# The opening of batch 0: idle matmul counts, the place of two transpose groups, and the place of one product group

## The chip, the core and the metric

The kernel runs on one core of one Trainium2 chip. A core has a matrix engine (TensorE, with its weight loads shown apart in the profile as PEld), VectorE (DVE), ScalarE (ACT), GpSimd (POOL) and SyncE (SP), each of which takes its instructions in order from its own program, and 16 DMA engines that bring data from the chip's main memory. Engines tell each other of finished work through semaphores. The metric is the time of one execution on the device, in microseconds (us), as the median of several runs. Results of matmuls go to a memory of their own, PSUM, from where VectorE or ScalarE must copy them before a matmul or a DMA can use them.

## The reference

Linear attention with a cosine reweighting, followed by a feed-forward layer; q, k and v have shape (8, 8, 576, 64) in float32, that is 8 batches, 8 heads, 576 positions and 64 features.

```python
def _attn_ref(q, k, v):
    theta = np.pi / 2.0 * pos / S
    def phi(x, c, s):
        r = np.maximum(x, 0.0)
        return np.concatenate([r * c, r * s], axis=-1)
    q_p = phi(q, cos_w, sin_w)
    k_p = phi(k, cos_w, sin_w)
    kv = np.einsum('bhsf,bhsd->bhfd', k_p, v)
    z = np.sum(k_p, axis=2)
    num = np.einsum('bhsf,bhfd->bhsd', q_p, kv)
    den = np.einsum('bhsf,bhf->bhs', q_p, z)[..., None] + 1e-06
    return (num / den).astype(np.float32)

def _moe_ref(x, w_in, w_out):
    h = x @ w_in
    g = h * (1.0 / (1.0 + np.exp(-1.702 * h)))
    return (g @ w_out).astype(np.float32)
```

The attention's output is laid out as 4608 rows (batch and position) of 512 columns (head and feature); w_in is 512 x 2048 and w_out 2048 x 512. The output is 4608 x 512 in float32.

## The kernel before

The kernel goes through the eight batches one after the other. For each batch it makes the features of k and q (relu, times a cosine and a sine, function `trig`), the matrix k^T v with the column sums of k beside it (`kv_mm`, copied out of PSUM by `kv_evac`), the quotient for five chunks of 128 positions (`num_mm` on TensorE, `num_div` on VectorE), a transpose of the quotient (`xturn_mm` on TensorE and `xturn_evac` on ScalarE in batch 0), and then the two layers (`mm1` with `gelu`, `mm2`). In the steady part the attention of the next batch is placed among the matmuls of the present one, so TensorE always has work. There is no scheduler: each engine's order is the order in which the kernel's text calls it (`manual_schedule`), and the semaphore waits follow from the tiles that an instruction reads and writes.

Batch 0 has no earlier batch to hide behind. Its order is written out by hand from line 375 to line 415:

- `idle` issues matmuls on a tile of zeros, whose results nobody reads: 12 with 512 columns, 100 with 64 columns (lines 375 and 376), and three more with 512 columns at line 392.
- The features of k (`trig(kr, kf, j)`, j = 0 to 8) are shared between VectorE and ScalarE (`act=True`).
- Line 385 makes the column sums of k, with `ones` as the moving side: 72 matmuls of one column.
- `qturn_pe(c)` transposes the features of q for chunk c on TensorE: 8 transposes, 4 for c = 4. `qevac(c)` copies them to `qT`, on VectorE, or on ScalarE with `act=True`. Transposes and the products of the first layer share a pool of four PSUM buffers (`pmm`, tiles named `mm`); tiles are given out in turn, so turn 3 takes turn 0's buffer and turn 4 takes turn 1's.
- `kv_mm(0, 2, ...)` and `kv_mm(2, 4, ...)` make the two halves of k^T v, 36 matmuls each (2 pairs of heads, 9 position slots, 2 heads). v comes by two DMAs from POOL's queue, one for each half (line 130).
- The two halves, the five quotient products and the transposes of the quotients share a second pool of two PSUM buffers (`pat`, tiles named `at`). `num_mm(c)` takes the buffer of `num_mm(c - 2)` once that chunk's quotient was transposed in it and copied out by `xturn_evac`. `num_mm(0)` reads both halves of k^T v: heads 0 to 3 the first, heads 4 to 7 the second.
- `start_block(0)` (line 346) then turns the quotients of chunks 0 and 1, makes the product of chunk 2, and goes over chunks c = 0 to 3 with 16 matmuls of the first layer each (`mm1_part`), with the later products and turns between them.

After that come the loads of batch 1, from POOL's queue, and the rest of the first layer of batch 0.

Of the kernel before, what the change touches and what calls it, by code (L numbers as in the profile page):

```python
# [19 lines left out]
def kernel(  # L20
# [117 lines left out]
    def trig(dst, src, j, act=False):  # L138
        i = src[:, :, ts(j, 64)]
        for cs, w in enumerate((cosw, sinw)):  # L140
            o = dst[:, j, :, ts(cs, 64)]
            if act:
                nc.scalar.activation(o, i, AF.Relu, scale=w[:, j:j + 1])
            else:
                nc.vector.tensor_scalar(o, i, 0.0, w[:, j:j + 1], op0=MAX, op1=MUL)  # L145
# [24 lines left out]
    def qturn_pe(c, home=None):  # L170
        tp = pmm.tile([128, 2, NI, 128], BF16, name="mm") if home is None else home
        for j in range(2 * c, min(2 * c + 2, NS)):
            for i in range(NI):
                nc.tensor.transpose(tp[:, j % 2, i], qn0[:, j, i, :], ident)  # L174
        tps[c] = tp

    def qevac(c, act=False):
        n = min(2 * c + 2, NS) - 2 * c
        o = qT[:, :, ds(c * 128, n * 64)].rearrange("f h (j p) -> f j h p", j=n)
        i = tps.pop(c)[:, 0:n].rearrange("f j i (hh p) -> f j (i hh) p", hh=2)  # L180
        if act:
            nc.scalar.activation(o, i, AF.Copy)
        else:
            nc.vector.tensor_copy(o, i)
# [20 lines left out]
    def kv_mm(i0, i1, rhs, col, n):  # L205
        for i in range(i0, i1):
            for j in range(NS):
                for hh in range(2):
                    r = slice(hh * 64, hh * 64 + 64)
                    nc.tensor.matmul(st["kv", i][:, hh, ds(col, n)], kr[r, j, i, :], rhs(r, i, j),  # L210
                                     start=(j == 0), stop=(j == NS - 1))

    def kv_evac(i0, i1):
        o = st["kvs"][:, :, i0:i1, 0:65]
        nc.vector.tensor_copy(o, st["ps", i0].rearrange("p hh (i e) -> p hh i e", e=65))  # L215
# [3 lines left out]
    def num_mm(c):  # L219
        ps = pat.tile([128, 2, 512], F32, name="at")  # L220
        for h in range(H):
            i, hh = divmod(h, 2)
            nc.tensor.matmul(ps[:, h // 4, ds((h % 4) * 65, 65)], qT[:, h, ts(c, 128)],  # L223
                             st["kvs"][:, hh, i, 0:65], start=True, stop=True)
        nums[c] = [ps]

    def num_div(c):
        ps = nums[c][0]
        pv = ps[:, :, 0:260].rearrange("p a (h e) -> p a h e", h=4)
        den = small.tile([128, 2, 4], F32, name="den")  # L230
        nc.vector.tensor_scalar(den, pv[:, :, :, 64], 1e-6, None, op0=ADD)  # L231
        inv = small.tile([128, 2, 4], F32, name="inv")
        nc.vector.reciprocal(inv, den)  # L233
        xn = small.tile([128, 2, 4, 64], BF16, name="xn", bufs=4)
        nc.vector.tensor_tensor(xn, pv[:, :, :, 0:64],  # L235
                                inv.unsqueeze(3).to_broadcast([128, 2, 4, 64]), op=MUL)
        nums[c].append(xn)
# [7 lines left out]
    def x_open(b):  # L245
        x[b] = xpool.tile([128, KC, S], BF16, name="xT")

    def xturn_mm(c):
        ps, xn = nums[c]
        xv = xn.rearrange("p a h e -> p (a h e)")  # L250
        for kc in range(KC):
            o = ps[:, kc // 2, ds(264 + (kc % 2) * 64, 64)].bitcast(BF16)
            nc.tensor.transpose(o, xv[:, ts(kc, 128)], ident)  # L253

    def xturn_evac(b, c):
        ps = nums.pop(c)[0]
        n = 128 if c < 4 else 64
        i = ps[:, :, 264:392].bitcast(BF16).rearrange("p a (k t) -> p a k t", k=2)[:, :, :, 0:n]
        o = x[b][:, :, c * 128:c * 128 + n].rearrange("p (a k) t -> p a k t", a=2)
        nc.scalar.activation(o, i, AF.Copy)  # L260
# [11 lines left out]
    def mm1_part(b, fc, t0, t1):  # L272
        if t0 == 0:
            hp[fc] = pmm.tile([128, MT], F32, name="mm")
        for kc in range(KC):
            nc.tensor.matmul(hp[fc][:, t0:t1], w_in_of(kc, fc), x[b][:, kc, t0:t1],  # L276
                             start=(kc == 0), stop=(kc == KC - 1))

    def gelu(fc):
        g = gpool.tile([128, MT], BF16, name="g")  # L280
        nc.scalar.activation(g, hp.pop(fc), AF.Gelu_apprx_sigmoid)  # L281
        gT[fc] = g

    def mm1(b, fc):
        mm1_part(b, fc, 0, MT)
        gelu(fc)
# [48 lines left out]
    def idle(n, cols=512):  # L335
        w = pmm.tile([128, 512], F32, name="mm")
        for _ in range(n):
            nc.tensor.matmul(w[:, 0:cols], warm[:, 0:128], warm[:, 0:cols], start=True, stop=True)  # L338
# [7 lines left out]
    def start_block(b, opened=False):  # L346

        if not opened:
            xturn_mm(0)
            xturn_evac(b, 0)  # L350
            xturn_mm(1)
            xturn_evac(b, 1)
            num_mm(2)
            num_div(2)
        for c in range(4):
            for fc in range(4):
                mm1_part(b, fc, c * 128, c * 128 + 128)
            if c == 0:
                num_mm(3)
                num_div(3)  # L360
                xturn_mm(2)
                xturn_evac(b, 2)
            if c == 1:
                num_mm(4)
                num_div(4)
                xturn_mm(3)
                xturn_evac(b, 3)
        for fc in range(4):
            gelu(fc)
        mm1(b, 4)  # L370
        xturn_mm(4)
        xturn_evac(b, 4)


    idle(12)
    idle(100, 64)
    for j in (0, 1):
        trig(kr, kf, j)
    for j in (2, 6, 7, 8):
# [17 lines left out]
        trig(qn0, qf0, j, act=True)  # L397
    qevac(0)
    trig(qn0, qf0, 8)
    qevac(1, act=True)  # L400
    qevac(2, act=True)
    kv_mm(0, 2, vb_rhs, 0, 64)
    kv_evac(0, 2)
    kv_mm(2, 4, vb_rhs, 0, 64)
    kv_evac(2, 4)
    qturn_pe(3)
    qevac(3, act=True)
    num_mm(0)
    num_div(0)
    num_mm(1)  # L410
    num_div(1)
    qturn_pe(4)
    qevac(4)
    x_open(0)
    start_block(0)


# [61 lines left out]
    num_div(2)  # L479
    mm2(0, 3, 12, 16)  # L480
    start_block(1, opened=True)


# [78 lines left out]
```

## Time and profile before

| what | us |
|---|---|
| median of 3 runs | 295.21 |
| all three runs | 295.99, 295.21, 295.20 |
| the profiled execution, its own time | 295.72 |
| its span, from the first to the last instruction | 294.0 |

The profile's shares are averages over stages with different limits, so the span is cut into the stages of the opening and the rest:

```profile
0.00:8.90 8.90, 7.64 (x112) 4.61 (x112) 4.93 (x19) 6.89 (x14) 4.81 (x16) 1.00 0.82 273
8.90:12.33 3.43, 3.38 (x113) 2.86 (x112) 2.64 (x9) 3.43 (x9) 0.00 (x0) 1.00 1.21 207
12.33:13.41 1.08, 0.00 (x1) 0.00 (x0) 0.00 (x0) 1.08 (x2) 0.21 (x2) 1.00 1.25 207
13.41:15.30 1.89, 1.89 (x83) 1.84 (x83) 0.86 (x2) 0.43 (x2) 1.89 (x3) 1.00 1.24 205
15.30:17.54 2.24, 0.84 (x17) 0.50 (x13) 2.09 (x7) 1.39 (x2) 2.24 (x5) 1.00 1.24 208
17.54:19.63 2.09, 2.01 (x40) 1.89 (x41) 1.57 (x6) 0.60 (x1) 1.19 (x2) 1.00 1.25 205
```

Each row is a stretch of the span in us, its length, and the busy time with the number of instructions of TensorE, its weight loads, VectorE, ScalarE and POOL; then the granted share of TensorE's clock, the busy share of the DMA engines and the rate in GB/s. Up to 8.90 us TensorE runs the idle matmuls. From 8.90 to 12.33 it makes the column sums and q's first three turns. From 12.33 to 13.41 it does nothing, then k^T v, and from 15.30 to 17.54 it is busy for 0.84 of 2.24 us while VectorE works on the first two quotients.

### The profile page before, as it was taken

How to read it: one execution, taken by the hardware profiler on the slowest of the kernel's cores; microseconds unless marked ns; L12 is line 12 of the kernel's file. 1: busy time of each engine (PE TensorE's matmuls, PEld its weight loads, DVE VectorE, ACT ScalarE, POOL GpSimd, SP SyncE). 2: the span in 40 equal slices, each digit the busy share in tenths (PEclk: the TensorE clock that was granted, in tenths of full speed). 3: DMA queues.
4: the chain of work that ended last, by engine and by line, in shares of the span. 5: the costliest groups of instructions: out<-in, count | busy, mean ns of one | idle time of the engine just before them, and what ended most of it. 6: DMA issues, size and time to landing. Idle time of an engine off the chain costs nothing.

```text
span 294.0 us, 6250 instructions
## 1 busy us (share of the span) xinstructions
PE 284.8 (97%) x2552; PEld 161.9 (55%) x2587; DVE 126.1 (43%) x362; ACT 131.5 (45%) x230; POOL 34.7 (12%) x68
## 2 busy tenths in 40 slices
PE   8879999999999999999999999999999999999995
PEld 4775656857454555455545554555455545565444
DVE  4674514693264825581567156725763420000000
ACT  7847653685104631463136412651175117773111
POOL 6260031500123001100110011000100010000000
PEclk9999999999999999999999999999999999999999
DMA  7999979596178965797469936995595240000322
GB/s 255 238 222 283 372 192 362 169 139 184 38 139 254 296 182 136 213 311 211 111 199 338 223 90 183 328 221 131 144 371 110 74 116 36 3 0 2 88 90 71
DMA packets 67228, 52.38 MB, mean 178 GB/s; under 512 B 47392, under 2 KB 57376, under 8 KB 67200
## 3 DMA queue, kind: packets, MB, share of 16 engines
q1 hardware_dynamic: 59824, 32.52, 43.2%
q0 software_dynamic: 7376, 19.47, 23.2%
q8 instruction: 20, 0.33, 0.4%
q14 instruction: 8, 0.07, 0.1%
HBM read 36.70 MB, written 9.44 MB: 157 GB/s over the span
## 4 chain that ended last, share of the span: by engine, by line
PE 95%; ACT 1%; issue 1%; DVE 1%; ACTq 0%
PE mm L326 42%; PE mm L276 36%; PE at L210 4%; PE mm L294 4%; PE at L223 3%; PE mm L338 3%; PE mm L303 2%; ACT g L281 1%; PE at L253 1%; DVE xn L235 1%; PE at L174 1%; PE mm L174 1%; DVE inv L233 0%; DVE den L231 0%; ACT ysb L330 0%
## 5 line engine op out<-in xcount | busy, mean ns | idle before, releaser
L326 PE MATMUL mm<-w_out_sb,g 128*128 128x512 bf16 (+1 forms) x506 | 116.2, 372 | 1.3 <-issue 0.2
L276 PE MATMUL mm<-xT,w_in 128*128 128x512 bf16 (+1 forms) x598 | 112.7, 345 | 0.5
L281 ACT ACTIVATE g<-mm 128x512 bf16<-128x512 f32 x128 | 75.6, 598 | 31.9 <-PE mm L276 31.9
L276 PEld LDWEIGHTS <-w_in 128*128 128x128 bf16 x608 | 61.8, 114 | 49.0
L326 PEld LDWEIGHTS <-g 128*128 128x128 bf16 x528 | 48.7, 98 | 49.5
L330 ACT ACTIVATE ysb<-mm 128x512 f32<-128x512 f32 (+1 forms) x37 | 21.7, 586 | 111.4 <-PE mm L326 111.4
L333 POOL DMA_DIRECT2D out_dram<-ysb x38 | 20.7, 548 | 177.2 <-ACT ysb L330 177.1
L145 DVE TENSOR_SCALAR kr<-kf,cosw 128x256 bf16<-128x256 f32 x68 | 23.7, 348 | 27.3 <-DMA kf<-in_k_dram 27.3
L235 DVE TENSOR_TENSOR xn<-at,inv 128x512 bf16<-128x512 f32 x40 | 27.7, 692 | 1.6 <-DVE inv L233 0.2
L145 DVE TENSOR_SCALAR kr<-kf,sinw 128x256 bf16<-128x256 f32 x68 | 23.8, 350 | 0.0
L231 DVE TENSOR_SCALAR den<-at 128x8 f32<-128x8 f32 x40 | 6.7, 166 | 36.9 <-PE at L223 36.9
L215 DVE CAST kvs<-at 128x520 bf16<-128x520 f32 (+1 forms) x9 | 5.8, 642 | 33.1 <-PE at L210 33.0
L223 PEld LDWEIGHTS <-qT 128*128 128x128 bf16 x320 | 14.5, 97 | 7.3
L223 PE MATMUL at<-kvs,qT 128*128 128x65 bf16 x320 | 15.9, 193 | 0.0
L158 DVE TENSOR_SCALAR qn<-qf,sinw 128x512 bf16<-128x512 f32 (+1 forms) x30 | 14.3, 477 | 0.0
L158 DVE TENSOR_SCALAR qn<-qf,cosw 128x512 bf16<-128x512 f32 (+1 forms) x30 | 14.3, 477 | 0.0
L210 PEld LDWEIGHTS <-kr 64*128 64x128 bf16 x648 | 10.2, 94 | 3.5 <-issue 3.2
L294 PE MATMUL mm<-xt,w_in 128*128 128x384 bf16 x64 | 10.6, 326 | 0.0
L326 PE MATMUL mm<-w_out_sb,gl_t 128*128 128x512 bf16 x47 | 10.5, 379 | 0.1
L338 PE MATMUL mm<-warm 128*128 128x64 bf16 (+1 forms) x114 | 8.5, 237 | 1.3 <-DVE warm L76 1.3
L294 PEld LDWEIGHTS <-w_in 128*128 128x128 bf16 x64 | 7.2, 113 | 3.3
L295 ACT ACTIVATE gl_t<-mm 128x384 bf16<-128x384 f32 x16 | 7.9, 491 | 2.4 <-PE mm L294 2.4
(60 smaller groups left out, 122.7 us busy)
## 6 DMA issues: line engine op xcount, KB each, us to landing
kf<-in_k_dram SPq DMA_DIRECT2D x5, 1152.0 KB, 6.5
vf<-in_v_dram SPq DMA_DIRECT2D x5, 1152.0 KB, 9.5
qf<-in_q_dram SPq DMA_DIRECT2D x5, 1024.0 KB, 5.7
out_dram<-ysb POOLq DMA_DIRECT2D x20, 256.0 KB, 2.6
kf<-in_k_dram POOLq DMA_DIRECT2D x2, 1152.0 KB, 10.2
vf<-in_v_dram POOLq DMA_DIRECT2D x2, 1152.0 KB, 13.7
out_dram<-ysb POOLq DMA_DIRECT2D x18, 128.0 KB, 3.2
w_in<-in_moe_w_in_dram POOLq DMA_DIRECT2D x4, 512.0 KB, 9.2
```

What stands on the lines that cost most here:

```text
L145: nc.vector.tensor_scalar(o, i, 0.0, w[:, j:j + 1], op0=MAX, op1=MUL)
L158: nc.vector.tensor_scalar(o, i, 0.0, sc, op0=MAX, op1=MUL)
L210: nc.tensor.matmul(st["kv", i][:, hh, ds(col, n)], kr[r, j, i, :], rhs(r, i, j), start=(j == 0), stop=(j == NS - 1))
L223: nc.tensor.matmul(ps[:, h // 4, ds((h % 4) * 65, 65)], qT[:, h, ts(c, 128)], st["kvs"][:, hh, i, 0:65], start=True, stop=True)
L235: nc.vector.tensor_tensor(xn, pv[:, :, :, 0:64], inv.unsqueeze(3).to_broadcast([128, 2, 4, 64]), op=MUL)
L276: nc.tensor.matmul(hp[fc][:, t0:t1], w_in_of(kc, fc), x[b][:, kc, t0:t1], start=(kc == 0), stop=(kc == KC - 1))
L281: nc.scalar.activation(g, hp.pop(fc), AF.Gelu_apprx_sigmoid)
L294: nc.tensor.matmul(hps, w_in_of(kc, fc), xt[:, kc, :], start=(kc == 0), stop=(kc == KC - 1))
L326: nc.tensor.matmul(yp[t, c0][:, c0:c1], w, w_out_sb[:, fc, c0:c1], start=(fc == 0), stop=(fc == FC - 1))
L330: nc.scalar.activation(ysb[:, c0:c1], yp[t, c0][:, c0:c1], AF.Identity)
L333: eng.dma_start(out=dst[:, c0:c1], in_=ysb[p0:p0 + n, c0:c1])
L338: nc.tensor.matmul(w[:, 0:cols], warm[:, 0:128], warm[:, 0:cols], start=True, stop=True)
```

## The change

Four edits, all in the opening of batch 0. There is one wide idle matmul less and 22 narrow ones more. `qevac(1)` goes from ScalarE to VectorE. The turns 3 and 4 of q, which stood after the second half of k^T v and after the second quotient, stand between the two halves, and `kv_evac(0, 2)` comes after turn 3. In `start_block` the product and the quotient of chunk 2 come ahead of the turn of chunk 1's quotient; `start_block(1)` is called with `opened=True` and doesn't run these lines.

```diff
@@ -348,10 +348,10 @@
         if not opened:
             xturn_mm(0)
             xturn_evac(b, 0)
+            num_mm(2)
+            num_div(2)
             xturn_mm(1)
             xturn_evac(b, 1)
-            num_mm(2)
-            num_div(2)
@@ -372,8 +372,8 @@
-    idle(12)
-    idle(100, 64)
+    idle(11)
+    idle(122, 64)
@@ -397,20 +397,20 @@
         trig(qn0, qf0, j, act=True)
     qevac(0)
     trig(qn0, qf0, 8)
-    qevac(1, act=True)
+    qevac(1)
     qevac(2, act=True)
     kv_mm(0, 2, vb_rhs, 0, 64)
+    qturn_pe(3)
+    qevac(3, act=True)
     kv_evac(0, 2)
+    qturn_pe(4)
+    qevac(4)
     kv_mm(2, 4, vb_rhs, 0, 64)
     kv_evac(2, 4)
-    qturn_pe(3)
-    qevac(3, act=True)
     num_mm(0)
     num_div(0)
     num_mm(1)
     num_div(1)
-    qturn_pe(4)
-    qevac(4)
     x_open(0)
     start_block(0)
```

## The prediction

> **What bounds the kernel now.** I read the shares of the span and the granted clock, then TensorE's timeline of the first 24 us, the chain of waits over the same stretch, the other engines' timelines there, and the DMA queues.
>
> ```profile
> PE 284.8 (97%) x2552; PEld 161.9 (55%) x2587; DVE 126.1 (43%) x362; ACT 131.5 (45%) x230; POOL 34.7 (12%) x68
> ...
> 24.00:290.70 266.70, 264.70 (x2135) 146.39 (x2165) 112.10 (x318) 114.38 (x198) 23.85 (x42) 1.00 0.64 173
> ```
>
> The first line is the page's, the second the stretch from 24 us to the last matmul: TensorE (second figure) works 264.7 of 266.7 us at clock 1.00. Nothing of the change lies there, so a shift at 24 us reaches the end undiminished, and no more. The idle time lies before:
>
> ```profile
> 3.79 5.18 PE L338 MATMUL mm<-warm 128*128 128x512 bf16 x106
> 8.91 1.05 PE L210 MATMUL at<-ones,kr 64*128 64x1 bf16 x72
> 9.89 1.07 PE L174 MATMUL mm<-ident,qn 128*128 128x128 bf16 x16
> 10.79 0.81 PE L338 MATMUL mm<-warm 128*128 128x512 bf16 x2
> 11.44 0.61 PE L174 MATMUL mm<-ident,qn 128*128 128x128 bf16 x8
> 11.98 0.35 PE L210 MATMUL at<-vb,kr 64*128 64x64 bf16 x12
> 13.41 1.07 PE L210 MATMUL at<-vb,kr 64*128 64x64 bf16 x60 [1.08 <-issue]
> 14.41 0.62 PE L174 MATMUL mm<-ident,qn 128*128 128x128 bf16 x8
> 14.87 0.65 PE L223 MATMUL at<-kvs,qT 128*128 128x65 bf16 x16
> 15.36 0.39 PE L174 MATMUL mm<-ident,qn 128*128 128x128 bf16 x4
> 16.50 0.40 PE L253 MATMUL at<-ident,xn 128*128 128x128 bf16 x4 [0.76 <-DVE xn L235]
> 17.54 0.40 PE L253 MATMUL at<-ident,xn 128*128 128x128 bf16 x4 [0.64 <-DVE xn L235]
> 17.77 0.41 PE L223 MATMUL at<-kvs,qT 128*128 128x65 bf16 x8
> 18.02 1.06 PE L276 MATMUL mm<-xT,w_in 128*128 128x128 bf16 x16
> 18.91 0.41 PE L223 MATMUL at<-kvs,qT 128*128 128x65 bf16 x8
> ```
>
> Start and duration in us; the bracket is idle time before the row. Three gaps: 1.08 in the middle of k^T v, with no releaser named, and 0.76 and 0.64 before turns of xn. From 17.5 us on TensorE runs without a gap, so the end hangs on when the products of chunk 1 (L276, second group, 19.63) start.
>
> **The gap without a releaser** decides the forecast. It comes after 12 of 72 matmuls, and matmul 13 waits for no semaphore; the next wait, for v's second half (landed 13.14), stands 24 matmuls later. The DMA queues tell more:
>
> ```profile
> q8 instruction: 20, 0.33, 0.4%
> q8 instruction: 1, 0.02, 30.5%
> ```
>
> Packets, MB and share of 16 engines: the first line is the page's, the second the stretch 11.0 to 11.2 us alone; the next such packets start only in 16.4 to 16.7 and 22.3 to 22.5. One packet is 0.33 MB / 20 = 16 KB and lasts 0.4% of 16 engines x 294 us / 20 = 0.94 us, so the first ended near 12.1. TensorE's program has 5,176 instructions, 259 for each packet. Ahead of matmul 13 stand 112 + 72 + 16 + 3 + 8 + 12 pairs of load and matmul and one load: 447, about two blocks less some 65 that the program's listing doesn't show. My reading, an inference: at 12.33 TensorE ran out of loaded instructions and waited for the block fetched at 11.1. Then the gap sits at an instruction's number, not at a piece of work. [...]
>
> **The change, part by part** (us; spacings are from start to start).
>
> *Idle matmuls.* The 11th and 12th wide ones already ran at full clock (weight loads at 5.46 and 5.68: 0.216 each; cold ones 0.427). 100 narrow ones take 8.90 - 5.90 = 3.0, 0.029 each (64 columns). 22 x 0.029 - 0.216 = +0.43: the idle stretch ends at 9.33. If the gap stays behind it, this costs nothing at once, for the gap swallows it. But it puts 42 instructions ahead: instruction 448 is then the last of the three wide matmuls of idle(3), since (11 + 122 + 72 + 16 + 2) pairs + 1 load = 447. TensorE gets there at 9.33 + 1.89 + 0.43 = 11.65 (from 8.90 to 10.79 in the rows, then two at 0.216).
>
> *When it goes on.* The request for the block was made while the idle matmuls ran; with one wide fewer the same instruction number comes 0.216 - 0.029 = 0.19 earlier. The loads it competes with are issued by SP and POOL, whose order doesn't change. So 13.41 - 0.19 = 13.22, and the gap grows to 1.57. Bounds: 11.65 (no wait) and 13.84 (the request moves with the idle stretch's end, +0.43). I take 13.22, nearest to the measured row.
>
> *Work now behind the gap.* One idle matmul 0.22, turn 2 of q 0.46 (8 transposes, 14.41 to 14.87), and 12 matmuls more of k^T v (60 in 1.00: 0.0167 each). From 13.22: 0.22 + 0.46 + 36 x 0.0167 = 0.60 gives 14.50.
>
> *Turns 3 and 4 between the halves.* 0.46 + 0.23 = 0.69, to 15.19; second half 0.60, to 15.79. Turn 3 was on the path already, but there it hid the evacuation of the second half; turn 4 filled the gap before xn. Now nothing lies between the last k^T v matmul and num_mm(0), whose heads 4 to 7 need that evacuation: matmul's own length 0.19, copy 0.43 to 0.48 (L215: two in 0.96), hand-overs 0.07, four matmuls 0.29: 1.00 from 15.79, against 15.29 - 14.41 = 0.88 with turn 3 inside. num_mm(0) ends at 16.79, not 15.29: +1.50. The first half's evacuation stands alone on VectorE and hides behind turns and second half, and turn 4's copy (0.41) between the two: VectorE is free from 15.76, 0.2 before the second half is done.
>
> *qevac(1) to VectorE* (0.69 for that shape): VectorE has nothing to do from 11.77 to 13.98, so nothing; if late it would hold turn 4, which takes its buffer. ScalarE comes to turn 2's copy sooner by 0.95; that isn't needed before 19. No DMA issue moves: SP's and POOL's orders are the same.
>
> *num_mm(2) ahead of turn 1.* In the chain of waits num_mm(2) sits behind turn 1, which waits for xn of chunk 1 until 17.49. From the end of num_mm(0): first xn +1.15, turn 0 to +1.61, its copy on ScalarE (0.03 + 0.60) to +2.24, num_mm(2) from +2.29 to +2.70, its xn 1.13 + 0.02 later, +3.85; turn 2 at +3.90. TensorE meanwhile: num_mm(2) 0.25, turn 1 0.23, chunk 0's products 0.89, num_mm(3) 0.25: +3.91. Turn 2 0.23: chunk 1 starts at +4.14, against 19.63 - 15.29 = 4.34: -0.2. The new wait is num_mm(2)'s for turn 0's copy; turn 1 queues behind it and has its data by then. Turn 1's copy now ends at +3.57, 0.09 ahead of num_mm(3), which takes that buffer: without that cover 0.1 or so is lost.
>
> *Sum:* +1.5 - 0.2 = +1.3. Against its own execution: 295.72 (span 294.0 and 1.7 around it) to 297.0. That execution stood 0.5 above the median, so for the median 295.21 + 1.3 = **296.5**. With the bounds of the block's arrival: -0.26 (11.65) to +1.9 (13.84).
>
> **Rivals.**
>
> *B, the gap belongs to k^T v* and ends at 13.41 whatever the count. Then TensorE is at it by 12.33 + 0.20 and goes on with 24 matmuls to 13.81, turns to 14.50, second half to 15.10, num_mm(0) to 16.10: +0.81 - 0.2 = +0.6, 295.8. For it: other landings cluster there (v at 13.14). Against: no wait in the program, and nothing landing at 13.41.
>
> *C, the block is there when it's asked for*, not slower. From 11.65: idle 0.22, turn 2 0.46, first half 0.60, turns 0.69 (13.62, v's second half long there), second half 0.60, 1.00: 15.22, -0.07 - 0.2 = -0.26: 294.95. It decides if the fetch comes over 1.3 us earlier than 13.22. For it: three times spread by 0.8 and the profiled run is 0.5 over their median, so the stall may be shorter in timed runs. Against: the request moves by 0.19 only. Were the stall gone in both kernels, the old one would wait for v's second half and end num_mm(0) at 13.20 + 0.60 + 0.88 = 14.68, and the new one is 0.54 - 0.2 = +0.35 behind: 295.6.
>
> *D, the clock falls.* Between 11.65 and 19 TensorE would idle 1.57, about 0.4 and 0.9 before the turns, and 0.7 for num_mm(2): over a third. Half clock for as long as the start ran cold (1.27 to about 5.4, 4.1 us) loses half of that, 2.0: +3.3, 298.5. Against: with gaps of 1.08, 0.76 and 0.64 the clock stayed at 1.00. [...]
>
> **Chances.** Forecast 0.60, B 0.12, C and its variant 0.16, D 0.06, what I don't see 0.06. The forecast's own range is 296.0 to 296.9. A difference under 0.3% (0.89 us: 294.3 to 296.1) can't be told from none. Slower: 0.55 of the forecast, 0.06 of D, 0.02 of the rest: 0.63. Same: 0.05 of the forecast, 0.12 of B, 0.13 of C: 0.30. Faster: 0.03 of C with all its luck, 0.04 unseen: 0.07; even all three gaps gone is only 2.5 us. Range 294.9 to 297.3: C's figure below, the late block above; D and some of C and the unseen fall outside.
>
> **What would show it.** Right: the gap without a releaser stands ahead of the last of three wide idle matmuls, from about 11.65 to 13.2, and k^T v has none; num_mm(0) ends near 16.8; chunk 1 starts near 20.9 and the stretch after is as dense as before. Wrong: a gap still inside k^T v (B), none over 0.5 us before 14 (C), matmul spacing doubled after 13 us (D), or a new gap past 24 us.

## The result, and the profile after

The changed kernel takes 299.44 us (median of 4 runs, 298.90 to 299.69) against 295.22 beside it: a ratio of 1.0134, 95% interval 1.0113 to 1.0155. It is slower by 4.2 us. Run again later, beside other runs of the kernel before, it took 299.69 against 296.23: 1.0112 [1.0097, 1.0127].

TensorE's timeline of the opening after the change (start, duration, and idle time before the row in brackets, in us):

```profile
3.79 6.32 PE L338 MATMUL mm<-warm 128*128 128x512 bf16 x127
10.04 1.05 PE L210 MATMUL at<-ones,kr 64*128 64x1 bf16 x72
...
11.93 0.59 PE L338 MATMUL mm<-warm 128*128 128x512 bf16 x2
13.92 0.38 PE L338 MATMUL mm<-warm 128*128 128x512 bf16 x1 [1.39 <-issue]
...
16.73 0.30 PE L223 MATMUL at<-kvs,qT 128*128 128x65 bf16 x4
17.32 0.52 PE L223 MATMUL at<-kvs,qT 128*128 128x65 bf16 x12 [0.30 <-DVE kvs L215]
18.82 0.40 PE L253 MATMUL at<-ident,xn 128*128 128x128 bf16 x4 [0.98 <-DVE xn L235]
19.91 0.40 PE L223 MATMUL at<-kvs,qT 128*128 128x65 bf16 x8 [0.69 <-ACT xT L260]
20.14 0.39 PE L253 MATMUL at<-ident,xn 128*128 128x128 bf16 x4
20.37 1.70 PE L276 MATMUL mm<-xT,w_in 128*128 128x128 bf16 x16
21.86 0.65 PE L223 MATMUL at<-kvs,qT 128*128 128x65 bf16 x8
22.32 0.62 PE L253 MATMUL at<-ident,xn 128*128 128x128 bf16 x4
22.73 1.67 PE L276 MATMUL mm<-xT,w_in 128*128 128x128 bf16 x16
24.23 0.41 PE L223 MATMUL at<-kvs,qT 128*128 128x65 bf16 x8
24.48 0.39 PE L253 MATMUL at<-ident,xn 128*128 128x128 bf16 x4
24.70 2.99 PE L276 MATMUL mm<-xT,w_in 128*128 128x128 bf16 x36
```

The gap without a releaser stands ahead of the last of the three wide idle matmuls, and k^T v has none. That was forecast. What was not: the 16 products of chunk 0 take 1.70 us, where they took 1.06 before. The transposes after them take 0.62 instead of 0.40. The same stretch cut at 6.93, 20.59 and 24.00 us, where the granted clock changes, and in steps of 3.41 us between (length, TensorE's busy time and number of matmuls, granted clock, DMA share, GB/s):

```profile
6.93:10.34 3.41, 3.41 (x132) 1.00 1.15 301
10.34:13.76 3.42, 2.19 (x80) 1.00 1.23 207
13.76:17.17 3.41, 3.11 (x97) 1.00 1.24 208
17.17:20.59 3.42, 1.60 (x32) 1.00 1.24 205
20.59:24.00 3.41, 3.41 (x39) 0.50 1.12 353
```

The clock came up at 6.93 us, and for one stretch of 3.41 us, 20.59 to 24.00, it was granted at half. From 6.93 to 20.59 are four times 3.41 us, so I call each such stretch of 3.41 us, counted from where the clock came up, a window. In the window just ahead of the fall TensorE was busy for 1.60 us. The same cut for the kernel before, whose clock came up at 5.41 and did not fall:

```profile
12.24:15.65 3.41, 2.33 (x96) 1.00 1.24 206
15.65:19.06 3.41, 2.01 (x39) 1.00 1.24 207
```

Where the time went, from the starts of the same work in both timelines:

| | before | after | later by |
|---|---|---|---|
| first matmul after the idle stretch | 8.91 | 10.04 | 1.13 |
| gap without a releaser ends | 13.41 | 13.92 | 0.51 |
| num_mm(0) ends | 15.29 | 17.61 | 2.32 |
| turn of chunk 0 | 16.50 | 18.82 | 2.32 |
| products of chunk 1 | 19.63 | 22.73 | 3.10 |
| products of chunks 2 and 3 | 20.99 | 24.70 | 3.71 |
| last matmul ends | 290.72 | 294.43 | 3.71 |

Nothing is added after 24.7 us. Of 3.71 us, 0.51 is the later end of the gap, 1.81 the work that now lies behind it (2.32 - 0.51), and 1.39 the rest. There the product's move saves 0.2 (by the forecast's sum, and by the traces below), so the half clock costs about 1.6. The spans differ by 3.7 and the medians by 4.2, because the profiled execution of before stood 0.5 above its median.

### The profile page after: what moved, and what is told of

Same layout as the page of the kernel before. It is cut to its first block, busy times and chain, and to the rows that moved or that the text cites. A ratio compares the mean times of both kernels' runs of the same rounds, so it can differ in the third digit from the quotient of the medians.

```text
span 297.7 us, 6326 instructions
## 1 busy us (share of the span) xinstructions
PE 289.8 (97%) x2608; PEld 164.8 (55%) x2608; DVE 126.9 (43%) x363; ACT 130.6 (44%) x229; POOL 34.6 (12%) x68
## 4 chain that ended last, share of the span: by engine, by line
PE 97%; issue 1%; DVE 1%; ACT 0%; ACTq 0%
PE mm L326 42%; PE mm L276 38%; PE at L210 4%; PE mm L294 3%; PE at L223 3%; PE mm L338 3%; PE mm L303 1%; PE at L253 1%; PE mm L174 1%; PE at L174 1%; DVE xn L235 0%; ACT xT L260 0%; DVE kvs L215 0%; ACT ysb L330 0%; DVE warm L76 0%
## 5 line engine op out<-in xcount | busy, mean ns | idle before, releaser
L326 PE MATMUL mm<-w_out_sb,g 128*128 128x512 bf16 (+1 forms) x528 | 117.7, 372 | 0.0
L276 PE MATMUL mm<-xT,w_in 128*128 128x512 bf16 (+1 forms) x608 | 114.8, 349 | 0.0
L276 PEld LDWEIGHTS <-w_in 128*128 128x128 bf16 x608 | 63.1, 115 | 49.0
L338 PE MATMUL mm<-warm 128*128 128x64 bf16 (+1 forms) x136 | 9.8, 239 | 2.6 <-issue 1.4
L260 ACT ACTIVATE xT<-at 128x512 bf16<-128x512 bf16 (+1 forms) x10 | 5.6, 563 | 7.9 <-PE at L253 6.0
L294 PEld LDWEIGHTS <-w_in 128*128 128x128 bf16 x64 | 7.2, 113 | 3.3
```

Of the source, the lines that this page charges most:

```text
L294: nc.tensor.matmul(hps, w_in_of(kc, fc), xt[:, kc, :], start=(kc == 0), stop=(kc == KC - 1))
L326: nc.tensor.matmul(yp[t, c0][:, c0:c1], w, w_out_sb[:, fc, c0:c1], start=(fc == 0), stop=(fc == FC - 1))
```

## The experiments

All times are medians, with the kernel before beside each of three groups of runs, and each group on a chip of its own. It took 295.97 (31 runs) beside the old counts, the new counts alone, the product alone and both gaps filled; 296.23 (9) beside the changed kernel once more, the same idle time, no narrow matmuls and the last version; 295.75 (17) beside the turns alone, the first gap filled and the new order without the block wait. Taken together these runs of one unchanged kernel go from 295.2 to 296.7; the last section says what varies.

### The old idle counts

```diff
-    idle(11)
-    idle(122, 64)
+    idle(12)
+    idle(100, 64)
```

(on the changed kernel)

> The changed kernel with the idle counts of before (12 wide, 100 narrow); the other three edits stay. Theory (the gap sits at an instruction's number, and the clock falls when a window of 3.4 us is idle by more than about half): the gap without a releaser is again after 12 matmuls of k^T v, until about 13.4; num_mm(0) ends near 16.1; the order edits alone cost +0.6, that is 295.8, if the clock stays at 1.00, and near 297.5 if the two gaps around turn 0 still fall into one window and halve the clock for 3.4 us. Rival (the added idle matmuls are harmless, the order costs all 4.2): 299.4.

297.56 us, ratio 1.0046 [1.0030, 1.0063]. The timeline of its profiled execution, whose clock stayed at 1.00:

```profile
12.24 0.35 PE L210 MATMUL at<-vb,kr 64*128 64x64 bf16 x12
13.67 0.53 PE L210 MATMUL at<-vb,kr 64*128 64x64 bf16 x24 [1.07 <-issue]
...
16.14 0.52 PE L223 MATMUL at<-kvs,qT 128*128 128x65 bf16 x12 [0.30 <-DVE kvs L215]
17.64 0.40 PE L253 MATMUL at<-ident,xn 128*128 128x128 bf16 x4 [0.98 <-DVE xn L235]
18.72 0.40 PE L223 MATMUL at<-kvs,qT 128*128 128x65 bf16 x8 [0.69 <-ACT xT L260]
...
21.94 2.99 PE L276 MATMUL mm<-xT,w_in 128*128 128x128 bf16 x35
```

With the old counts the gap is back after 12 matmuls of k^T v. The three later gaps, 0.30, 0.98 and 0.69, are those of the changed kernel, so they belong to the order. The ten runs are of two kinds: four with a clock of 1.000 at 296.66 to 297.21, six with 0.992 to 0.994 at 297.53 to 298.02. The same program is about 1.1 us slower when its clock falls, and whether it falls varies from run to run. In the profiled execution a window edge, at 16.17, stood between the 0.30 gap and the other two, and the window kept 1.74 us busy:

```profile
16.17:19.58 3.41, 1.74 (x36) 1.00 1.25 207
```

Those that kept the clock stand 0.7 to 1.2 above the 295.97 beside them, where 0.6 was expected. By the traces the order costs 0.7: from the end of the gap to the products of chunks 2 and 3 it is 8.27 us here (13.67 to 21.94) and 7.58 before (13.41 to 20.99). The price of the half clock can be read too, since the order is the same: from the turn of chunk 0 to the products of chunks 2 and 3 it is 4.30 us here (17.64 to 21.94) and 5.88 in the changed kernel (18.82 to 24.70), 1.58 more.

### The new idle counts alone

```diff
-    idle(12)
-    idle(100, 64)
+    idle(11)
+    idle(122, 64)
```

(on the kernel before)

> The kernel before with the new idle counts alone (11 wide, 122 narrow). Theory: the gap moves ahead of the last of the three wide idle matmuls and ends 13.2 to 13.9; turn 2 and 12 matmuls of k^T v come behind it: +0.7 to +1.4, 295.9 to 296.6; the gaps before the turns of xn stay 0.75 and 0.64 and the clock stays at 1.00. Rival (the idle matmuls alone make the clock fall or cost most of the 4.2): 297.5 or more.

296.55 us, ratio 1.0028 [1.0014, 1.0041]; no run had a clock under 0.999.

```profile
11.36 0.38 PE L338 MATMUL mm<-warm 128*128 128x512 bf16 x1
13.41 0.38 PE L338 MATMUL mm<-warm 128*128 128x512 bf16 x1 [1.67 <-issue]
```

The idle counts move the gap by themselves and lengthen it. Its 1.67 us are too many: the second of the three wide matmuls has a weight load in the trace (at 11.36) but no record of its own, so about 0.22 of the gap is work and about 1.45 is left. The new counts cost 0.6 to 0.8, at the low end of the expected 0.7 to 1.4, and do not make the clock fall.

### The product of chunk 2 alone

```diff
+            num_mm(2)
+            num_div(2)
             xturn_mm(1)
             xturn_evac(b, 1)
-            num_mm(2)
-            num_div(2)
```

(on the kernel before)

> The kernel before with the one edit of start_block: the product of chunk 2 ahead of the turn of chunk 1. Theory: -0.2, 295.0, no different from before by what can be told; a gap of about 0.7 before that product takes the place of the 0.64 before turn 1; the clock stays at 1.00. Rival (this edit is what halves the clock, since its gap stands next to the one before turn 0): a stretch at clock 0.5 and 296.5 or more.

295.50 us, ratio 0.9995 [0.9978, 1.0011], and no run had a clock under 0.998.

```profile
16.25 0.40 PE L253 MATMUL at<-ident,xn 128*128 128x128 bf16 x4 [0.76 <-DVE xn L235]
17.34 0.40 PE L223 MATMUL at<-kvs,qT 128*128 128x65 bf16 x8 [0.69 <-ACT xT L260]
...
19.19 1.06 PE L276 MATMUL mm<-xT,w_in 128*128 128x128 bf16 x16
```

A gap of 0.69 ahead of the product takes the place of the 0.64. The expected -0.2 lies within the interval and is not shown by the times. The trace shows it: from the turn of chunk 0 to the products of chunk 1 it is 2.94 us here (16.25 to 19.19) and 3.13 before (16.50 to 19.63).

### The turns alone

```diff
-    qevac(1, act=True)
+    qevac(1)
...
+    qturn_pe(3)
+    qevac(3, act=True)
     kv_evac(0, 2)
+    qturn_pe(4)
+    qevac(4)
     kv_mm(2, 4, vb_rhs, 0, 64)
     kv_evac(2, 4)
-    qturn_pe(3)
-    qevac(3, act=True)
...
-    qturn_pe(4)
-    qevac(4)
```

(on the kernel before)

> The kernel before with the moved turns 3 and 4 and qevac(1) on VectorE, and nothing else. Theory: num_mm(0) ends 0.8 later because the second half's copy lies bare, no -0.2 from the product: +0.8, near 296.8 where the clock stays, and in some runs the clock falls (gaps of 0.30, 0.98 and 0.64 can share one window of 3.41 us, which leaves about 1.5 us busy), then near 297.9. Rival (the product's move is what makes the clock fall): never under 0.998.

297.73 us, ratio 1.0063 [1.0043, 1.0083]. Two of seven runs kept the clock (296.86 and 297.38), five had 0.992 to 0.994. So the moved turns, not the product, open the gaps that let the clock fall. They cost about 1.1 to 1.6 without a fall, somewhat more than the 0.8 of the sum.

### Filling the gaps

```diff
     num_div(1)
+    idle(4)
     x_open(0)
...
             xturn_evac(b, 0)
+            idle(3)
             num_mm(2)
```

(on the changed kernel; a further kernel has the first of these alone)

> The changed kernel with seven more wide idle matmuls where TensorE waits: four after num_div(1), ahead of turn 0, and three between turn 0 and the product of chunk 2 (0.216 us each, 0.86 and 0.65 in gaps of 0.98 and 0.69). Theory (idle time in one window halves the clock): it stays at 1.00 throughout and the time falls by about 1.6, to 297.8, though nothing else is mended. Rival (the clock falls for another reason, or its fall isn't what costs): 299.4 or a little more.

> The changed kernel with four wide idle matmuls ahead of turn 0 alone; the gap of 0.69 ahead of the product of chunk 2 stays open. Theory (a window of 3.41 us with less than about half of it busy halves the clock): the gaps left, 0.30, 0.1 and 0.69, leave 2.3 us busy, so the clock stays at 0.998 or more and the time is 297.2 to 297.6, as with both gaps filled. Rival (the gap right ahead of the product is what makes it fall): 0.992 to 0.994 and 299.

With both gaps filled 297.37 us, ratio 1.0052 [1.0037, 1.0067]; with the first alone 297.59, ratio 1.0051 [1.0030, 1.0071]. All fifteen runs had clocks of 0.998 or more; the 0.999 of the second kernel's profiled execution comes from half clock after its last matmul, from 295.08 us on. The stretches between window edges of the kernel with the first fill, whose clock came up at 4.95:

```profile
11.78:15.19 3.41, 2.02 (x57) 1.00 1.25 206
15.19:18.60 3.41, 2.87 (x64) 1.00 1.24 207
18.60:22.02 3.42, 2.86 (x60) 1.00 1.24 229
```

Four matmuls whose results nobody reads raise the busy time of the critical stretch to 2.87 us and take off about 1.8 us (ratio 1.0051 against 1.0112). The 0.69 gap before the product stays open in it and does no harm. What is left, 1.4 to 1.8 us, is what the moved gap and the order cost.

### The changed kernel once more

> The changed kernel itself once more, beside the others of this call. Theory (a moved block wait and order cost +1.4, as with the gaps filled, and the clock's fall about 1.7 to 2 more): in most runs a clock of 0.992 to 0.995 and 299.0 to 299.5; runs whose clock stays at 0.998 or more, if there are any, near 297.4. Rival (the difference to the run with the filled gaps came from the day and the chip): 297.4 whatever the clock.

299.69 us, ratio 1.0112 [1.0097, 1.0127]. All four runs had clocks of 0.992 to 0.994, as had the first four: no run kept it, so the theory's "near 297.4" was seen only in the filled kernels. The rival is out, since this ran beside the same kernel before.

```profile
12.64:16.05 3.41, 2.64 (x89) 1.00 1.24 207
16.05:19.46 3.41, 1.44 (x39) 1.00 1.24 206
19.46:22.88 3.42, 3.42 (x42) 0.50 1.19 280
```

### The same idle time with fewer instructions

```diff
-    idle(11)
-    idle(122, 64)
+    idle(14)
+    idle(100, 64)
```

(on the changed kernel)

> The changed kernel with three more wide idle matmuls (0.65 us) in place of the 22 more narrow ones (0.64): the same idle time, 38 instructions fewer. Theory (the gap sits at an instruction's number): it is back inside k^T v, after 10 matmuls of its first half, with no gap ahead of the wide idle matmuls, and the time is near that of the changed kernel with the old idle counts, 297.6. Rival (the gap follows from the longer idle stretch): it stays ahead of turn 2, 299.4.

297.83 us, ratio 1.0059 [1.0044, 1.0074].

```profile
12.00 0.32 PE L210 MATMUL at<-vb,kr 64*128 64x64 bf16 x10
13.41 0.56 PE L210 MATMUL at<-vb,kr 64*128 64x64 bf16 x26 [1.09 <-issue]
```

The gap is after 10 matmuls of k^T v, as the count of instructions says, though the idle time is that of the changed kernel. The window ahead of the fall, and the one after it:

```profile
14.81:18.22 3.41, 1.72 (x56) 1.00 1.24 207
18.22:21.64 3.42, 3.14 (x38) 0.50 1.24 209
```

The clock fell in three of four runs; the fourth took 297.73 with a clock of 1.000, hardly less than the others (297.77 to 298.29), and left no trace that would tell why.

### No narrow idle matmuls

```diff
-    idle(12)
-    idle(100, 64)
+    idle(26)
```

(on the kernel before)

> The kernel before with 26 wide idle matmuls and no narrow ones: about the same idle time at full clock (14 x 0.216 for 100 x 0.029), 172 instructions fewer. Theory: the first block boundary moves to the end of turn 4, which TensorE reaches near 15.3, and the block asked for near 9.5 to 9.9 is there by 15.2; the gap without a releaser goes, a wait for the second half of v (landing 13.1) of about 0.5 takes its place, num_mm(0) ends near 14.7 instead of 15.3: -0.6, 295.4 against a median of 295.97 in the last session. Rival (the gap is not the block's): it stays at k^T v and the time is 296.

294.49 us, ratio 0.9948 [0.9932, 0.9965]: faster than the kernel before by 1.5 us, with one line changed.

```profile
11.77 1.24 PE L210 MATMUL at<-vb,kr 64*128 64x64 bf16 x72
12.94 0.62 PE L174 MATMUL mm<-ident,qn 128*128 128x128 bf16 x8
13.40 0.66 PE L223 MATMUL at<-kvs,qT 128*128 128x65 bf16 x16
13.89 0.27 PE L174 MATMUL mm<-ident,qn 128*128 128x128 bf16 x2
14.95 0.27 PE L174 MATMUL mm<-ident,qn 128*128 128x128 bf16 x2 [0.78 <-issue]
15.06 0.38 PE L253 MATMUL at<-ident,xn 128*128 128x128 bf16 x4
```

The gap did not go, as expected, but moved to the same instruction number: after 26 + 72 + 16 + 3 + 8 + 72 + 8 + 16 + 2 = 223 pairs and a load, the 447 of before. There TensorE would have waited for the first quotient in any case: turn 0 follows at 15.06. The expected wait for the second half of v is missing; k^T v runs through.

### The new order without the block wait

```diff
-    idle(11)
-    idle(122, 64)
+    idle(26)
```

(on the changed kernel)

> The changed kernel with 26 wide idle matmuls in place of all of its first idle stretch: the order edits without a block wait on the path. Theory: the block boundary comes at the end of num_mm(1), where TensorE waits for the quotient anyway; num_mm(0) ends near 14.7 against 13.8 with the old order and the same idle matmuls: +0.8 - 0.2 = +0.6 on that kernel's 294.5, that is 295.1, and 296.7 in runs whose clock falls. Rival (the order edits are harmless once the block wait is gone): 294.3.

295.45 us, ratio 0.9984 [0.9971, 0.9997], no run under 0.998. Against 0.9948 with the old order and the same idle matmuls, measured in another group of runs, the new order costs about 0.0036 x 296 = 1.1 us, near twice the expected 0.6.

```profile
14.93 0.74 PE L223 MATMUL at<-kvs,qT 128*128 128x65 bf16 x12 [0.30 <-DVE kvs L215]
```

The gap after the same 447 instructions is there too, within this row: the weight load of its eleventh matmul starts at 15.20, the matmul itself at 15.46, and the row takes 0.74 us instead of 0.52. TensorE waits for the quotient right after it, so this costs nothing.

### A version that beats both

```diff
-    idle(12)
-    idle(100, 64)
+    idle(22)
...
     qevac(4)
+    idle(3)
     x_open(0)
...
             xturn_evac(b, 0)
+            idle(2)
+            num_mm(2)
+            num_div(2)
             xturn_mm(1)
             xturn_evac(b, 1)
-            num_mm(2)
-            num_div(2)
```

(on the kernel before)

> A version meant to beat both: 22 wide idle matmuls and no narrow ones, the product of chunk 2 ahead of turn 1, three wide idle matmuls ahead of turn 0 and two between turn 0 and that product, the rest as before. Theory: no block wait (-0.6), the product's -0.2, idle stretch shorter by up to 0.9 in runs that start long cold, clock at 1.00: 294.9 to 295.2 against 295.97, with less spread. Rival (the idle stretch is now too short and the clock falls, or the second half of v sets the time anyway): 296 or more.

294.43 us (294.19 to 294.45 in five runs), ratio 0.9938 [0.9925, 0.9950]. It is faster than the kernel before by 1.8 us and than the changed one by about 5, and its runs spread by 0.3 us where those of before beside it spread by 0.8, and all of them by 1.5. Whether it also beats the one-line version can't be told: the intervals overlap.

## Why the prediction was right in part and wrong in the sum

- **The gap without a releaser** was read rightly. In all thirteen profiles, with 112, 133, 114, 26 and 22 pairs in the first idle stretch, it stood after 447 instructions, and it followed the count and not the work (10, 12, 72 or no matmuls of k^T v ahead of it) or the idle time. That a block of the program was late is still an inference. In the two kernels the gap ended 1.3 and 1.5 us after the first instruction packet did (13.41 after 12.08 in the kernel before, 13.92 after 12.39 in the changed one), but no run shows where a block ends: two packets at the forecast's own 259 are 518 instructions, 71 more than 447, and its "some 65" rests on no row. B has nothing left to stand on.
- **The terms behind the gap.** Work from the gap's end to the end of num_mm(0) took 3.69 us (13.92 to 17.61), forecast 3.57. With the clock kept from falling, the change costs 1.4 to 1.8 against the +1.3 of the forecast.
- **The end of the gap** was forecast at 13.22 and came at 13.92, but the cold start was longer in that execution: the clock came up at 6.93 and not 5.41. Until the clock came up the idle matmuls went at half the pace (in the kernel before weight loads 0.427 apart, and 0.216 after it): half of those 1.52 us is 0.76, and 13.22 + 0.76 is 13.98. Where it came up at 5.81, in the second profile of the changed kernel, the gap ended at 13.41, and the same sum gives 13.42. So the sum of the forecast held in both, and it took the cold start of one execution for a constant. No trace shows a request for the block or what it depends on, so the 0.19 in that sum stays an inference; measured are the start of the first instruction packet, 11.10 and 11.49, and the end of the gap.
- **The product's move**: -0.2 expected, -0.19 in the traces, too small for the times.
- **The step that failed** is rival D, put at 0.06 with the argument that "with gaps of 1.08, 0.76 and 0.64 the clock stayed at 1.00". The clock fell in eight of eight runs, and neither of the two profiles has a gap over 1.7 us. What the falls went with is the share of a window that is busy: 1.44, 1.60 or 1.72 us of 3.41 in the window ahead of each, with no gap over 0.98 in it, and 1.74 or more in the other windows of the opening. The three gaps that the new order puts within 2.9 us (0.30, 0.98, 0.69) add up to 1.97 and leave 1.44 of 3.41 where one window holds them all. Where an edge cuts into them, more is left: 1.60, 1.72 or 1.74. The rows for that sum stood in the prediction, and the price (+2.0 of half clock for 4.1 us) was of the right kind: 3.41 us at half clock cost about 1.6 in the trace.
- **Chances and range.** Slower was right. The range ended at 297.3 because D lay outside it; D's own 298.5 was the closest of the figures.

## What to carry to other kernels

Where a stretch is bound by waits, add up TensorE's busy time over windows of 3.4 us before you move work: here each window with 1.44 to 1.72 of its 3.41 us busy was followed by one at half clock, which cost 1.6 us, and four matmuls that compute nothing got that back. Count instructions, not only time, in idle fill: 26 wide matmuls in place of 112 mixed ones moved a 1.08 us stall to a place where TensorE waited anyway, and with that one line the kernel was 1.5 us faster. Where the end of a stall is set by something else, work that moves from ahead of it to behind it adds its full length: with the new counts alone the gap ended at 13.41, as before, about 0.88 us of work by the forecast's spacings (0.22 + 0.46 + 12 x 0.0167) had moved behind it, and the products of chunk 1 started 0.94 later (20.57 against 19.63).

## What the runs showed of the hardware

- **The threshold.** By the modelled busy time, windows of 3.41 us with 1.44, 1.60 and 1.72 us busy in the opening were each followed by one window at half clock. Windows with 1.74, 1.79, 1.97 and 2.01 were not. The window that holds the last matmul of each program is a further case: with 0.31 to 1.37 us busy (five profiles) half clock followed, with 1.78 to 2.66 (seven) it did not, but neither did it with 1.58 in the kernel with the same idle time and fewer instructions. The limit lies near half, and these busy times do not place it better than 1.58 to 1.74 us.
- **The start of full clock moves.** It came at 3.96 to 6.93 us in the thirteen profiles, although TensorE's first weight load started at 1.25 in both kernels. With the old idle counts the idle stretch ended at 8.56 where full clock came at 4.72, and at 9.16 where it came at 5.93. That, I take it, is why runs of the unchanged kernel differ by up to 1.5 us: half of 2.97 us is 1.5.
- **The gap ends on a grid.** In the thirteen profiles it ended at 12.90, 13.16 or 13.17, 13.41 (four times), 13.67 (twice), 13.92, 14.95, 15.21 and 15.46 us: steps of 0.256 us or multiples of it, to within 0.01. The times of the kernel before, where everything later hangs on the gap's end, lie on such steps too: near 295.2, 295.5, 295.7, 296.0, 296.2, 296.5 and 296.7 us in all 57 runs. No run tells why there is a grid.
- **A block's packet may hold up data.** POOL's first instruction that needs the second half of v started at 13.20 in the kernel before, whose first instruction packet started at 11.10, and at 12.10 in the kernel with 26 wide idle matmuls, whose packet started at 12.64, after v. In the other two kernels without narrow idle matmuls the packet came after v too, and that instruction started at 12.34 and 12.71; in the other nine kernels the packet came first, and it started at 13.00 to 13.65. That the packet held the data up would explain the missing wait for v, but it is a guess: no run tested it by itself.
